# K's builds with low positions as weights, K's rows moved inside SBUF, and a new written-out order

## The chip, the cores and the metric

The kernel runs on one core of one Trainium2 chip. The metric is device time of one execution in microseconds (us), the median of three runs. A profiled execution of the kernel before gives the trace; its times are counted from the first instruction of the span.

## The reference

Two independent results stand side by side in one output of 2048 x 896 (bfloat16).

The first 448 columns are linear attention with 16 heads of 28: `qkv = x @ wqkv`; q and k go through a head's 28 x 28 matrix, then both softmaxes of it and of its negative make 56 features; the output is `phi_q (phi_k^T v) / (phi_q sum(phi_k))`, times `wo`.

The last 448 columns are a long convolution. For each of 448 channels a filter K of 2048 positions is a sum over 256 complex states, and the signal u is convolved with it:

```python
P = jnp.exp(logdA[:, :, None] * l[None, None, :])
K = jnp.einsum("dn,dnl,dn->dl", Cc, P, dB).real
...
Yf = Uf * Kf[None, :, :, :]
y = irfft2(Yf)[..., :L] + u * Dskip
```

`logdA` and `dB` come from the inputs by `dt = exp(log_dt)`. The positions `l` are rounded to bfloat16, so that large ones repeat.

## The kernel before, in words

**Stages.** The signal's spectrum is made by matmuls with tables (`signal_spectrum`, L593) and parked in DRAM. Attention runs as 16 key tiles (`key_tile`, L742), an end of the keys (`key_end`, L774), and four query stretches (`query`, L784) of 512 rows. K is made in eight blocks of 56 channels (`NCHK`), in three groups (`GROUPS`, L36: blocks 0 to 3, then 4 and 5, then 6 and 7). When a group's K is there, its spectrum follows (`kernel_spectrum`, L864), then the product with the signal's spectrum (`conv_group`, L948) and the inverse (`inverse`, L921).

**How a block of K is made.** A position is a high part (32 values, `HI`) plus a low part (49 values, `LO`), so K at (h, lo) is a sum over states of U at h times W at lo. `dampings` and `rotations` make W for the 49 low positions with ScalarE's exponentials and sines, after groups of 16 matmuls (`phases`); `damp` multiplies the two on VectorE. `hi_tables` (L698) makes U for the 32 high positions in five levels, each two products and a sum. The sum is an accumulating DMA that GpSimd issues for the (block, level) pairs in `ADD_BY_DMA` (L97: blocks 1 to 6), and otherwise an add on VectorE. `build_k` (L723) then makes one block in two builds of 112 matmuls: for each of 7 channels, four terms (two halves of the states, real and imaginary) and four groups g of channels, with U's 32 high positions as weights and W's 49 low positions streaming, each group in a tile of 32 columns of the array (`tile_position=(0, 32 * g)`). A build's 128 x 343 result is evicted into `Ts`, whose partition is 32g + h and whose free axes are lo and channel. Both operands of a build's matmul are read with a step of a whole row of 112 or 224 elements.

**How K's rows are put in place.** The spectrum wants `Kt`: 5 tiles of 128 partitions, one partition a position, in the order `K_ROWS` (L33) gives. `scatter_k` (L842) writes the group's `Ts` to a DRAM tensor `KD` by four DMAs (step `kd`), then reads `KD` back into `Kt` by eight DMAs and into `KZ` by two (step `sc`), and multiplies one row of `KZ` (step `last`). DMAs go out on SyncE's or GpSimd's queue.

**What sets the order.** Nothing is scheduled on the chip or by the compiler: each operation is a unit with a number, and `ORDER` (L100) lists all units with the engine each runs on (P, D, A, G, S for TensorE, VectorE, ScalarE, GpSimd, SyncE). `HOMES` (L158) fixes the bytes of each tile in SBUF and `BANKS` the PSUM bank of each result. A search made these lists from the costs that the helpers carry (`tt`, `act`, `copy`, `dma`: L327 to L382); the costs have no other effect. Waits follow from the data, and each engine takes its own units strictly in the listed order. All vector operations have the line of their helper: L330 products and sums, L340 activations, L350 evictions, L359 matmuls, L381 DMAs.

Of the kernel before, what the change touches and what calls it, by code (L numbers as in the profile page):

```python
# [9 lines left out]
BF16 = mybir.dt.bfloat16  # L10
# [10 lines left out]
NQ = 14  # L21
CW = 4 * NQ
# [10 lines left out]
K_ROWS = [(0, 0, 0, 8, (9, 25, 1), 1), (1, 0, 0, 8, (25, 41, 1), 1), (2, 0, 8, 16, (10, 41, 2), 1), (3, 0, 16, 24, (1, 8, 1), 0),  # L33
          (3, 56, 16, 24, (8, 41, 4), 0), (4, 0, 24, 32, (0, 8, 2), 0), (4, 32, 24, 32, (8, 41, 8), 0), (4, 72, 24, 32, (41, 48, 1), 0)]
# [9 lines left out]
def _row_positions():  # L44
    pos = {}
    for kt, r, h0, h1, run, low_first in K_ROWS:
        hl = [(h, lo) for h in range(h0, h1) for lo in range(*run)]
        if low_first:
            hl = [(h, lo) for lo in range(*run) for h in range(h0, h1)]
        for i, (h, lo) in enumerate(hl):  # L50
            pos[kt, r + i] = HI[h] + LO[lo]
    return pos
# [44 lines left out]
ADD_BY_DMA = {(k, lv) for k in range(1, 7) for lv in range(5)}  # L97
# [3 lines left out]
15G 0S 24P 8A 154G 1A 85P 2S 5S 81P 4A 25A 26D 87P 6S 88D 199G 27P 23D 86D 83P 7A 49P 84D 3A 33A 16G 82D 51P 29A 34D  # L101
155G 19G 54P 52A 56D 153S 50A 31A 57D 53P 30A 58D 156D 10S 13S 12S 60D 32A 55D 59D 157D 28P 38A 41A 37A 46A 43A 35A
44A 97P 190P 168P 40A 39D 47A 169A 18S 183P 664P 113P 36D 98A 184A 665A 45D 175P 667A 666A 200G 42D 99P 100A 115P 116D
176A 48D 669A 198S 160P 161A 119P 193P 120D 61D 101P 661P 194A 102D 668A 191A 114A 62D 662A 201D 195P 196A 131P 170P
663A 64D 171A 172S 69A 173P 158P 174A 185P 197S 132D 71A 9S 117P 240P 241A 238P 239A 135P 63D 186A 70A 73D 75A 210P
202D 72D 136D 66D 133P 118A 211A 20G 178P 89P 93P 159A 162S 94A 205P 103P 104D 179A 21S 220P 22S 65D 76A 206A 90D 230P
78D 74A 203P 77D 204A 129P 221A 130D 228P 231A 229A 232S 68D 67D 79A 180P 95P 682S 163P 673P 96D 127P 80A 181A 728S
134D 208P 209A 683D 730D 681A 212S 684D 218P 729D 242S 680A 225P 226A 698G 91P 223P 164A 678A 685D 687D 676A 128A 188P
189A 731G 686D 674A 92D 215P 192S 688D 137P 213P 224D 216A 207S 214A 732D 139P 733D 219A 233P 234A 235P 222S 677A 236A
141P 679A 138A 690D 689D 675A 165P 691D 693D 701D 123P 140A 124A 700D 166A 125P 187S 692D 126A 142A 237S 694D 143P  # L110
734G 736D 144A 670P 671A 696D 121P 716P 122A 177S 735D 717A 243P 276P 167S 718A 672A 227S 246A 265P 268A 182S 245A
695D 699D 702D 707P 709A 708A 11S 710P 697D 737G 739D 738D 740G 217S 775D 821D 254P 257A 279A 711A 256A 719P 713A 267A
705P 703P 278A 712A 765P 715A 14S 714A 726A 720A 249D 250D 744G 723A 722A 774S 721A 769A 724A 260D 105P 727A 790G 282D
742D 725A 244P 248A 770A 776D 704A 777G 283D 766A 706A 741D 266P 743G 17G 773A 261D 753P 247G 771A 762P 746D 106D 745D
779D 768A 767A 269G 772A 309P 778D 780G 270A 748D 747D 763A 271D 764A 756P 758A 749P 751P 251D 755A 782D 781D 783G
760A 750D 761A 754A 312A 972D 255P 107P 757A 791D 752A 822D 253P 108A 311A 298P 259A 820S 109P 110A 300A 301A 272D
258G 299P 792D 303A 799P 287P 793D 800A 784D 759A 785D 262D 252P 273D 823G 289A 824D 825D 304D 786G 801A 111P 826G
263P 264P 787D 802P 290A 302G 788D 321P 794D 112A 805A 291G 274P 325A 803A 320P 275P 288P 828D 277P 310P 323A 293D
804A 315D 806A 807A 281A 322A 314A 292A 827D 811P 789G 313G 305D 818A 817A 316D 829G 294D 808P 795P 815A 810A 797P
814A 809A 306D 971S 962P 295D 812A 838D 317D 796A 280G 284D 286P 297P 973D 974G 285P 813A 296P 967A 819A 326D 308P  # L120
963A 970A 830D 831D 307P 318P 964A 354P 816A 837D 975D 959P 966A 965A 358A 976D 798A 836G 832G 968A 397P 319P 324G
969A 961A 327D 343P 833D 960A 328D 950P 834D 840D 347A 951A 977G 365P 839D 952A 369A 332P 978D 331P 979D 334A 835G
333A 337D 953P 957A 956A 1018D 958A 988D 841P 400A 954A 843P 335G 842A 399A 338D 401G 955A 980G 999P 403D 1019D 844A
353P 1001A 1017S 1000A 355A 982D 981D 329P 847S 336A 342P 356A 989D 375P 991D 378A 983G 1002A 990D 398P 402A 1004A
357G 339D 985D 377A 984D 1003A 408P 1020G 411A 364P 330P 340P 341P 387P 410A 367A 344A 845G 345A 391A 386P 389A 996P
997A 376P 998A 409P 1021D 1022D 368G 414D 388A 846G 366A 359D 346G 348D 1008P 413A 360D 392D 1005P 1010A 986G 349D
1009A 380A 370D 1014A 1023G 1024D 848G 987G 1025D 1006A 1007A 381D 1026G 992P 993A 361D 994P 404D 1129D 1119P 350D
351P 352P 415D 1130D 1016A 371D 382D 995A 393D 1013A 1116P 390G 363P 1012A 1121A 405D 412G 379G 1122A 1011A 372D 362P
373P 1027D 1128S 145S 383D 374P 385P 1015A 1127A 1033G 428P 1028D 1131G 1126A 1124A 1120A 152S 1144G 394D 396P 407P
1035D 1029G 384P 425P 395P 1118A 151S 1133D 851G 849S 416D 1132D 1123A 1134G 1117A 1125A 418P 406P 1034D 417P 881S  # L130
426A 1153P 1107P 1030D 1155A 1031D 1154A 1032G 1109A 427A 1037D 1156P 1108A 1036D 858G 431P 430A 1136D 1135D 893S
1110P 429A 1038P 420D 1137G 432A 1115A 433A 1112A 1146D 1111A 1158A 422D 1114A 863S 419D 1039A 1113A 1175D 1157A 1040P
423D 852G 424D 1160A 1174S 1145D 1176D 1161A 1139D 1159A 434P 435A 489P 1041A 492P 490A 1138D 1140G 453P 486P 436A
455P 494A 547P 1147D 1043S 443P 421D 454A 493A 437P 1044S 1148D 850S 1141D 880S 1142D 465P 491A 456A 473P 856G 463P
444A 488A 855G 464D 487A 475P 859D 466A 438D 439D 440D 1177D 1179D 1178D 854G 476A 483P 899S 1143G 857S 485A 484A 905S
1162P 474A 1045G 853G 1180D 445P 446A 513P 1165P 1172A 1181D 514A 1169A 874S 1164A 495P 1163A 904S 1149P 496D 1151P
862S 1182D 497D 887S 1042S 521P 1166A 522A 1150A 882P 869S 1183D 1168A 1184D 883A 1170A 864P 1185D 441D 1186D 886S
442D 892S 1167A 898S 894P 1152A 888P 1187D 1173A 1188D 875S 1051S 477D 1171A 1055G 531P 532A 876P 889A 865A 1047S 906P
907A 868S 895A 877A 884P 503P 504A 1192D 501P 502A 885A 1050G 861S 908P 900P 870P 871A 890P 1053S 909A 1046S 523P 533P
150S 891A 1052G 146S 1054G 511P 498D 512A 1048S 1191D 872P 860G 550P 901A 1189D 896P 897A 534A 1049S 1193D 1190G 878P  # L140
879A 1194D 552A 551A 1056D 524A 478P 1195P 1196A 1197P 479A 902P 1198A 1200G 499D 1201G 500D 903A 515D 548A 447D 866P
1199S 602P 603A 910D 535D 536P 537A 149S 549A 604A 505D 867A 599P 911D 1202S 1204S 1212G 1206S 1211G 467D 147S 525D
526P 600A 148S 544P 457D 458P 873A 912D 545A 448P 449A 1207G 601A 913D 459A 516P 541P 468P 469A 929D 930D 517A 1205S
527A 1203G 608P 542A 605P 1071P 610A 1210G 543A 1072A 916D 928D 1063P 1064A 1067P 506P 1208S 914D 931D 1213D 1068A
1065P 559P 480P 1059P 915D 609A 932D 1066A 481A 546A 606A 607A 518P 507A 933D 935D 528P 450P 451A 519A 1073P 529D 553P
1074A 934D 1060A 1057S 569P 1224P 570A 936D 659S 452S 1239D 470P 1209S 1061P 1062A 937D 1069P 471A 1070A 1220P 1221A
1216P 1217A 554D 591P 592A 917D 1228P 555D 556D 1058G 538P 1222P 460P 1225A 658S 589P 1082D 561P 657S 1223A 1226P
1218P 557D 1229A 461A 462S 938D 1230P 1076D 1219A 560A 520S 558D 923P 571P 508P 509A 562D 1231A 1227D 581P 1075D 563D
660S 582A 1077D 1078D 918P 590A 919A 572A 1215G 939D 593D 925P 1091D 1214G 579P 580A 583D 564P 1089D 942P 1080D 1100D
926A 617P 618A 1092D 539A 584P 945P 924A 1232D 947P 510S 565A 573D 1093D 948A 482S 1233D 920P 1235D 639P 1081D 574P  # L150
575A 566P 567A 1086P 1079D 585A 472S 627P 1234D 1237D 628A 1238D 1087A 640A 594P 595A 576P 586P 946A 649P 927S 587A
1236D 1240P 1241A 1249D 647P 940P 921A 1090D 1243P 568S 1094D 1095D 1096D 1099D 1097D 1101P 577A 578S 1247D 1251D 922S
# [124 lines left out]
def kernel(  # L277
# [65 lines left out]
    def acopy(out_, a):  # L343
        sbuf = 0 if isinstance(a, tuple) else 0.045
        plan.add({"ACT": 0.039 + sbuf + count(out_) * 0.8333e-3}, lambda e: nc.scalar.copy(at(out_), at(a)), [whose(a)], [out_])  # L345
# [696 lines left out]
```

## Time and profile before

| what | before |
|---|---|
| median of 3 runs | 311.49 us (311.19 to 312.22) |
| the profiled execution | 313.22 us, span 311.3 us |
| TensorE busy | 251.5 us, 4152 matmuls |
| VectorE busy | 265.3 us, 334 instructions |
| ScalarE busy | 239.8 us, 417 instructions |
| GpSimd busy | 55.2 us, 93 instructions |
| mean granted TensorE clock | 0.950 |
| DMA packets | 50233, 41.11 MB; 32467 under 512 bytes |

A row of a group reads: line, engine (PE TensorE's matmuls, PEld its weight loads, DVE VectorE, ACT ScalarE, POOL GpSimd, SP SyncE), operation, what it writes and reads, shapes and count, then busy time in us and the mean of one in ns, then the idle time of the engine just before and what ended it. For a matmul, 128*32 means 128 rows and 32 columns of weights. In rows of stretches, each engine has its busy us and in brackets the number of instructions alive in the stretch; then the granted clock, the share of the DMA engines and GB/s. In the chain of waits, each row has a start, a length and what took that time. In rows of DMA issues: count, KB each, median us to landing.

### The profile page before, as it was taken

What the parts mean: (1) busy time and instruction counts of PE and PEld (TensorE: products, weight loads), DVE (VectorE), ACT (ScalarE), POOL (GpSimd) and SP (SyncE); (2) the same over time, 40 slices, a digit from 0 to 9 for tenths busy, and PEclk for the clock granted to TensorE, in tenths of its full rate; (3) what the DMA queues carried; (4) which work ended last, traced back from release to release, by engine and by line L of the source; (5) the groups of instructions that cost most, each with busy time, mean ns of one, the idle gap of its engine ahead of it and who ended that gap; (6) DMA issues with size and microseconds to landing.
All of it is one profiled execution on the core that took longest, in us unless ns stands there. A gap on an engine that the chain in (4) does not pass through costs nothing.

```text
span 311.3 us, 9636 instructions
## 1 busy us (share of the span) xinstructions
PE 251.5 (81%) x4152; PEld 202.6 (65%) x4152; DVE 265.3 (85%) x334; ACT 239.8 (77%) x417; POOL 55.2 (18%) x93
## 2 busy tenths in 40 slices
PE   4539787966968989779997793999993999699994
PEld 3524454444847667475686672989973688588982
DVE  1399999989999898999999993979985977699683
ACT  2698999999999998988999992869793475307342
POOL 3003000111231222315332240230113310000000
PEclk9987999999799999999999997799998799879999
DMA  7684432786363645457957569569092896310254
GB/s 242 175 270 155 138 117 60 193 264 150 85 115 73 114 91 113 83 107 123 142 98 148 106 111 113 120 151 286 9 50 33 187 355 184 129 29 17 76 135 133
DMA packets 50233, 41.11 MB, mean 132 GB/s; under 512 B 32467, under 2 KB 46336, under 8 KB 49808
## 3 DMA queue, kind: packets, MB, share of 16 engines
q1 hardware_dynamic: 42384, 24.50, 30.7%
q0 software_dynamic: 6128, 14.83, 25.2%
q10 hardware_dynamic: 1680, 1.18, 1.4%
q8 instruction: 32, 0.52, 0.7%
q14 instruction: 9, 0.07, 0.1%
HBM read 20.29 MB, written 8.74 MB: 93 GB/s over the span
## 4 chain that ended last, share of the span: by engine, by line
PE 26%; DVE 20%; DMA 19%; ACT 7%; issue 5%; SPq 2%; DVEq 0%; ACTq 0%
PE psum L359 26%; DVE sbuf L330 18%; DMA sbuf<-sbuf 9%; ACT sbuf L340 4%; DMA KD<-sbuf 3%; DMA sbuf<-const 3%; ACT sbuf L350 2%; DMA out_dram<-sbuf 2%; SPq L381 2%; DVE sbuf L758 1%; DMA sbuf<-in_A_wo_dram 1%; DVE sbuf L764 1%; ACT L340 0%; DVE sbuf L806 0%; DVE sbuf L809 0%
## 5 line engine op out<-in xcount | busy, mean ns | idle before, releaser
L359 PE MATMUL psum<-sbuf 128*32 128x49 bf16 (+10 forms) x4056 | 247.1, 262 | 50.0 <-ACT sbuf L350 13.4
L359 PEld LDWEIGHTS <-sbuf 128*32 128x32 bf16 (+5 forms) x4056 | 195.4, 122 | 95.8 <-issue 48.2
L330 DVE TENSOR_TENSOR sbuf<-sbuf 128x896 bf16<-128x896 bf16 (+8 forms) x241 | 218.2, 954 | 32.9 <-DMA sbuf<-sbuf 8.9
L340 ACT ACTIVATE sbuf<-psum 128x448 bf16<-128x448 f32 (+4 forms) x213 | 137.4, 773 | 2.7 <-PE psum L359 2.6
L350 ACT CAST sbuf<-psum 128x448 bf16<-128x448 f32 (+3 forms) x171 | 90.1, 600 | 56.2 <-PE psum L359 49.9
L381 POOL DMA_DIRECT2D sbuf<-sbuf x30 | 25.7, 870 | 102.1 <-DVE sbuf L330 56.3
L340 ACT ACT_TABLE_LOAD x13 | 16.7, 1283 | 2.3 <-issue 2.1
L758 DVE TENSOR_REDUCE sbuf<-sbuf 128x32 f32<-128x896 bf16 x16 | 16.7, 1065 | 0.0
L381 POOL DMA_DIRECT2D sbuf<-KD x16 | 10.6, 706 | 21.1 <-DMA KD<-sbuf 21.1
L330 DVE TENSOR_TENSOR sbuf<-psum,sbuf 128x896 f32<-128x896 f32 (+4 forms) x14 | 9.0, 660 | 4.9 <-PE psum L359 4.6
L564 PE MATMUL psum<-sbuf 128*112 128x128 bf16 x64 | 6.7, 242 | 5.9 <-DMA sbuf<-in_A_x_dram 2.8
L564 PEld LDWEIGHTS <-sbuf 128*112 128x112 bf16 x64 | 6.1, 149 | 7.6 <-DMA sbuf<-in_A_x_dram 4.6
L350 DVE CAST sbuf<-psum 128x448 bf16<-128x448 f32 (+2 forms) x13 | 8.0, 629 | 2.0 <-PE psum L359 1.2
L381 POOL DMA_DIRECT2D KD<-sbuf x6 | 7.2, 1297 | 13.9 <-ACT sbuf L350 13.8
L695 POOL MEMSET sbuf<- 128x224 bf16 x8 | 3.8, 479 | 23.1 <-DVE sbuf L330 19.1
L350 DVE COPY sbuf<-psum 112x512 bf16<-112x512 bf16 (+1 forms) x16 | 6.3, 406 | 1.7 <-PE psum L564 1.5
L603 POOL DMA_INDIRECT sbuf<-in_B_u_dram,sbuf x2 | 3.2, 1593 | 25.3 <-DVE sbuf L330 25.1
L381 POOL DMA_DIRECT2D sbuf<-SUd x4 | 4.7, 1182 | 8.8 <-PE psum L359 6.4
L753 POOL MEMSET sbuf<- 128x16 bf16 x16 | 5.8, 451 | 2.5 <-DMA sbuf<-sbuf 2.5
L345 ACT CAST sbuf<-sbuf 128x1792 bf16<-128x1792 f32 x3 | 5.7, 1899 | 0.0
L350 ACT COPY sbuf<-psum 112x512 bf16<-112x512 bf16 (+1 forms) x8 | 5.2, 648 | 0.3 <-PE psum L564 0.3
L764 DVE RECIPROCAL sbuf<-sbuf 128x32 bf16<-128x32 f32 x16 | 5.0, 334 | 0.1
(20 smaller groups left out, 30.4 us busy)
## 6 DMA issues: line engine op xcount, KB each, us to landing
sbuf<-sbuf POOLq DMA_DIRECT2D x12, 448.0 KB, 4.4
sbuf<-sbuf POOLq DMA_DIRECT2D x18, 224.0 KB, 3.8
SUd<-sbuf SPq DMA_DIRECT2D x16, 224.0 KB, 2.1
sbuf<-const SPq DMA_DIRECT2D x3, 1024.0 KB
sbuf<-const SPq DMA_DIRECT2D x17, 160.0 KB, 4.3
out_dram<-sbuf SPq DMA_DIRECT2D x24, 112.0 KB, 4.8
sbuf<-sbuf SPq DMA_DIRECT2D x8, 224.0 KB
sbuf<-in_B_u_dram SPq DMA_DIRECT2D x2, 896.0 KB
```

Source lines behind the costliest of these rows:

```text
L330: lambda e: nc.vector.tensor_tensor(out=at(out_), in0=at(a), in1=at(b), op=op), [whose(a), whose(b)], [out_])
L340: lambda e: nc.scalar.activation(at(out_), at(a), func, scale=scale, bias=bias), [whose(a)], [out_],
L345: plan.add({"ACT": 0.039 + sbuf + count(out_) * 0.8333e-3}, lambda e: nc.scalar.copy(at(out_), at(a)), [whose(a)], [out_])
L350: lambda e: (nc.scalar.copy if e == "ACT" else nc.vector.tensor_copy)(at(out_), at(a)), [whose(a)], [out_])
L359: nc.tensor.matmul(out_, lhsT=lhsT, rhs=rhs, start=start, stop=stop, **kw)
L381: plan.add({e: own[e] for e in engs}, lambda e: QUEUES[e].dma_start(out=out_, in_=in_, **kw), r, w, mode=k, load=wire, lat=(1.0 if dram el ...
L564: mms(p, [lambda t, j=j, x=x: nc.tensor.transpose(t[:, j, :], x[:, 112 * j:112 * j + 112], ident[:, :]) for j in range(4)], 0.22, [x, iden ...
L603: plan.add({"POOL": 1.2}, lambda e: nc.gpsimd.indirect_dma_start(out=ub.rearrange("p s d -> p (s d)"), out_offset=None, in_=u8, in_offset= ...
L695: pool(0.2, lambda en: nc.gpsimd.memset(w[:, :, ZERO, :], float(np.sqrt(0.5))), [], [w[:, :, ZERO, :]])
L753: pool(0.2, lambda e: nc.gpsimd.memset(V[:, D_HEAD, :], 1.0), [], [V[:, D_HEAD, :]])
L758: plan.add({"DVE": 0.996}, lambda e: nc.vector.tensor_reduce(zk[:, :, :], EK[:, :, :].rearrange("p s (h f) -> p s h f", f=D_HEAD), axis=AX ...
L764: nc.vector.reciprocal(rk[:, :, :], zk[:, :, :])
```

## The change

- **Builds.** The operands change sides: W's 49 low positions are the weights, U's 32 high positions stream. `NQ` is 28 instead of 14, so that a block has two groups g of 28 channels instead of four of 14, each in a tile of 64 columns of the array. A build takes 14 channels instead of 7, still with 112 matmuls. Its result is 113 x 448, and `Ts` has partition 64g + lo and free axes h and channel.
- **K's rows.** `KD` is gone. Each of the 8 entries of `K_ROWS` goes for each of the two g straight from `Ts` to `Kt` by a DMA inside SBUF, and five more fill `KZ`: 21 for a group, where 14 were.
- **Sums by DMA.** `ADD_BY_DMA` now holds blocks 0 and 7 too, and group 0's two sums of products in `conv_group` are accumulating DMAs.
- **Costs, order, places.** The costs in the helpers are a few ns higher (VectorE 0.061 to 0.068 and the like); small DMA pieces cost 1.3 times as much there; a build's cost is left at 2.75. `ORDER`, `HOMES` and `BANKS` are new. Units on TensorE stay 315; VectorE has 337 (334 before), ScalarE 390 (409), GpSimd 111 (89), SyncE 132 (117).

```diff
-NQ = 14
-CW = 4 * NQ
+NQ = 28
+CW = 2 * NQ
...
-ADD_BY_DMA = {(k, lv) for k in range(1, 7) for lv in range(5)}
+ADD_BY_DMA = {(k, lv) for k in range(8) for lv in range(5)}
...
     def build_k(k, Ts, x0):
+        half = NQ // 2
         for hq in range(2):
             step(f"build{k}.{hq}")
-            p = ps([128, 7, N_LO])
+            p = ps([113, half, N_HI])
             calls = []
-            for qq in range(7):
-                q = 7 * hq + qq
+            for qq in range(half):
                 for i in range(4):
                     nch, ri = i // 2, i % 2
-                    for g in range(4):
-                        xc = nch * CW + g * NQ + q
+                    for g in range(2):
+                        xc = nch * CW + g * NQ + half * hq + qq
                         calls.append(lambda t, g=g, qq=qq, i=i, ri=ri, xc=xc: mm(
-                            t[32 * g:32 * g + 32, qq, :], U[k][:, :, ri, xc], W[k][:, ri, :, xc], i == 0, i == 3,
-                            tile_position=(0, 32 * g)))
+                            t[64 * g:64 * g + N_LO, qq, :], W[k][:, ri, :, xc], U[k][:, :, ri, xc], i == 0, i == 3,
+                            tile_position=(0, 64 * g)))
             mms(p, calls, 2.75, [U[k], W[k]], mode=1)
-            copy(Ts[:, :, x0 + 7 * hq:x0 + 7 * hq + 7], (p, lambda t: t.rearrange("p c l -> p l c")))
+            x = x0 + half * hq
+            copy(Ts[:, :, x:x + half], (p, lambda t: t.rearrange("p c h -> p h c")))
...
     def scatter_k(gi, Ts):
-        step(f"kd{gi}")
+        step(f"sc{gi}")
         c0, n = GROUPS[gi]
+        x = NQ * n
+        for g in range(2):
+            cs_ = slice(c0 * CW + x * g, c0 * CW + x * g + x)
+            for kt, r, h0, h1, (l0, l1, s) in K_ROWS:
+                d = Kt[r:r + (h1 - h0) * len(range(l0, l1, s)), kt, cs_]
+                dma(["SP", "POOL"], d, Ts[64 * g + l0:64 * g + l1:s, h0:h1, :], r=[Ts], w=[d])
+        step(f"last{gi}")
         cs_ = group_cols(gi)
-        x = NQ * n
-        for g in range(4):
-            v = Ts[32 * g:32 * g + 32, :, :]
-            dma(["SP", "POOL"], KD[gi][:, :, x * g:x * g + x].rearrange("l h x -> h l x"), v, r=[v], w=[("KD", gi, g)])
-        step(f"sc{gi}")
-        kd = [("KD", gi, g) for g in range(4)]
-        for kt, r, h0, h1, (l0, l1, s), low_first in K_ROWS:
-            m = (h1 - h0) * len(range(l0, l1, s))
-            d = Kt[r:r + m, kt, cs_]
-            v = KD[gi][l0:l1:s, h0:h1, :]
-            dma(["SP", "POOL"], d, v if low_first else v.rearrange("l h x -> h l x"), r=kd, w=[d])
         d = KZ[0:1, cs_]
-        dma(["SP", "POOL"], d, KD[gi][8, 0:1, :], r=kd, w=[d])
+        dma(["SP", "POOL"], d, Ts[8:73:64, 0, :], r=[Ts], w=[d])
         d = KZ[32:36, cs_]
-        dma(["SP", "POOL"], d, KD[gi][48, 31:32, :].to_broadcast([4, CW * n]), r=kd, w=[d])
-        step(f"last{gi}")
+        for j in range(4):
+            dma(["SP", "POOL"], KZ[32 + j:33 + j, cs_], Ts[48:113:64, 31, :], r=[Ts], w=[KZ[32 + j:33 + j, cs_]])
         tt(d, d, U4[32:36, cs_], ALU.mult)
...
         for i in range(2):
-            tt(a[i][:, :, :], a[i][:, :, :], c[i][:, :, :], ALU.add)
+            if gi == 0:
+                dma(["POOL"], a[i].rearrange("p a b -> p (a b)"), c[i].rearrange("p a b -> p (a b)"), r=[c[i]], w=[a[i]],
+                    max_dma_last_dim=3584, accum_op=ALU.add)
+            else:
+                tt(a[i][:, :, :], a[i][:, :, :], c[i][:, :, :], ALU.add)
         finish(1, *a)
```

More of the change, by code (lines that the diff above doesn't have):

```diff
@@ L45, in _row_positions @@
     pos = {}
[L46 to L50, printed above, removed]
+    for kt, r, h0, h1, run in K_ROWS:
+        for i, (lo, h) in enumerate((lo, h) for lo in range(*run) for h in range(h0, h1)):
             pos[kt, r + i] = HI[h] + LO[lo]
@@ L104 @@
[L104 to L113, printed above, removed]
@@ L199 @@
+6060207202036541254226737433735221545606020022672731367210251622004004206043441662322"
 class Plan:
@@ L338, in act @@
         sbuf = 0 if isinstance(a, tuple) else 0.045
-        plan.add({"ACT": 0.05 + sbuf + count(out_) * 0.8333e-3},
+        plan.add({"ACT": 0.056 + sbuf + count(out_) * 0.8333e-3},
                  lambda e: nc.scalar.activation(at(out_), at(a), func, scale=scale, bias=bias), [whose(a)], [out_],
@@ L344, in acopy @@
         sbuf = 0 if isinstance(a, tuple) else 0.045
-        plan.add({"ACT": 0.039 + sbuf + count(out_) * 0.8333e-3}, lambda e: nc.scalar.copy(at(out_), at(a)), [whose(a)], [out_])
+        plan.add({"ACT": 0.045 + sbuf + count(out_) * 0.8333e-3}, lambda e: nc.scalar.copy(at(out_), at(a)), [whose(a)], [out_])
     def copy(out_, a, rate=1.0417e-3):
         n = count(out_)
-        plan.add({"ACT": 0.039 + n * 0.8333e-3, "DVE": 0.065 + n * rate},
+        plan.add({"ACT": 0.052 + n * 0.8333e-3, "DVE": 0.07 + n * rate},
                  lambda e: (nc.scalar.copy if e == "ACT" else nc.vector.tensor_copy)(at(out_), at(a)), [whose(a)], [out_])
```

136 lines of the change are left out of this document (72 added, 64 removed), and 63 rows, old and new, of the table HOMES.

## The prediction

> **What bounds the kernel now.** I read the page's head first, then the busy time of the engines in stretches cut at the kernel's own marks: the first build of K (77.77 us), the first build of the last block (218.09), the last build's end (223.87), the end.
>
> ```profile
> PE 251.5 (81%) x4152; PEld 202.6 (65%) x4152; DVE 265.3 (85%) x334; ACT 239.8 (77%) x417; POOL 55.2 (18%) x93
> ```
>
> ```profile
> core 0: us, PE busy (x) PEld busy (x) DVE busy (x) ACT busy (x) POOL busy (x), PEclk, DMA share, GB/s
> 0.00:77.77 77.77, 53.20 (x452) 35.18 (x452) 64.64 (x72) 67.43 (x103) 8.44 (x16) 0.96 0.59 177
> 77.77:218.09 140.32, 117.71 (x2480) 98.24 (x2480) 128.38 (x168) 125.92 (x221) 38.48 (x67) 0.96 0.64 121
> 218.09:223.87 5.78, 5.78 (x227) 5.62 (x226) 5.78 (x6) 4.37 (x8) 0.00 (x0) 1.00 0.01 3
> 223.87:311.32 87.45, 74.77 (x996) 63.56 (x996) 66.50 (x91) 42.06 (x87) 8.23 (x10) 0.92 0.51 119
> sum 311.32, PE 251.46 PEld 202.59 DVE 265.30 ACT 239.78 POOL 55.15; mean PE 62.86 PEld 50.65 DVE 66.33 ACT 59.94 POOL 13.79
> ```
>
> No engine bounds all of it. In the middle stretch VectorE (128.4 of 140.3 us) and ScalarE (125.9) set the pace and TensorE has 22.6 us to spare; in the tail TensorE is the busiest with 74.8 of 87.5. So work added to TensorE is free in the middle until it has used those 22 us, and is paid in full afterwards. How close TensorE can come to fully busy, a denser stretch shows:
>
> ```profile
> 200.00:224.00 24.00, 23.44 (x578) 22.33 (x568) 21.91 (x30) 18.94 (x38) 3.77 (x6) 1.00 0.63 166
> ```
>
> That is 0.977, which I take as its ceiling. Last, the chain of waits (start, length, what) and the list of waits (total, times, longest), for what the trip of K through DRAM costs:
>
> ```profile
> 226.79 10.33 DMA KD<-sbuf
> ```
>
> ```profile
> PE psum L359 <- DMA sbuf<-in_A_wo_dram: 5.4, 2, 5.0
> ```
>
> The last group's write to DRAM stands in the chain with 10.3 us, but TensorE has other work then and stops for only 5.4 us (the wo load it names was issued on SyncE between K's transfers and landed behind them).
>
> **The builds, step by step.** Every block of K is two builds of 112 small matmuls: 16 x 112 = 1792. Before, four 32-column tiles of the array each hold 32 high positions as weights, and 49 low positions stream past. After, the sides are swapped: 49 columns of weights need a 64-column tile, so only two tiles fit, and 32 columns stream. The count stays 1792. What one costs depends on what bounds it now.
>
> ```profile
> L359 PE MATMUL psum<-sbuf 128*32 128x49 bf16 x1792 | 46.2, 279 | 7.0 <-DVE sbuf L330 2.5 <-DMA sbuf<-sbuf 1.7 <-issue 1.6
> L359 PEld LDWEIGHTS <-sbuf 128*32 128x32 bf16 x1792 | 43.8, 141 | 8.8 <-DVE sbuf L330 4.5 <-issue 4.0
> L359 PE MATMUL psum<-sbuf 128*128 128x112 bf16 x1016 | 59.2, 216 | 7.5 <-ACT sbuf L340 6.3 <-ACT sbuf L350 0.5 <-DMA sbuf<-const 0.3
> L359 PEld LDWEIGHTS <-sbuf 128*112 128x112 bf16 x256 | 17.6, 132 | 6.2 <-issue 2.9 <-DVE sbuf L330 1.2
> L359 PE MATMUL psum<-sbuf 112*128 112x8 bf16 x128 | 3.8, 166 | 0.0
> ```
>
> A 49-column matmul lasts 279 ns, a 112-column one 216, an 8-column one 166: by the last two a column costs 0.48 ns and 49 should last 186. The 93 ns more are the build's own, as are a load of 32 columns at 141 ns against 112 columns at 132. Both operands of a build are read one element at a time, 224 or 448 bytes apart. Next, the beginning of one build in slices of some 10 ns (x counts the matmuls alive), and whole builds at two granted clocks:
>
> ```profile
> 94.52:94.53 0.01, 0.00 (x1) 1.00 0.00 0
> 94.53:94.54 0.01, 0.01 (x4) 1.00 1.83 358
> 94.54:94.59 0.05, 0.05 (x4) 1.00 1.82 358
> 94.59:94.60 0.01, 0.01 (x4) 1.00 0.00 0
> 94.60:94.61 0.01, 0.01 (x5) 1.00 3.66 717
> ...
> 94.63:94.65 0.02, 0.02 (x8) 1.00 0.91 179
> ...
> 77.77:80.50 2.73, 2.73 (x113) 2.73 (x116) 2.73 (x5) 2.73 (x6) 1.14 (x2) 0.65 0.53 149
> ...
> 94.50:97.20 2.70, 2.67 (x113) 2.70 (x116) 2.70 (x4) 2.69 (x4) 0.00 (x0) 1.00 0.11 20
> ```
>
> Four matmuls, one for each tile, start within 20 ns; then nothing starts for 60 ns, until the first tile takes its next. So the queue can hand out matmuls much faster than they run, and a tile's own chain (load, stream, next) is the limit. A build takes 2.7 us, 24.1 ns a matmul, 96.4 ns for one round of four tiles. It takes 2.73 us at a granted clock of 0.65 too, so the round isn't array cycles; it looks like reading.
>
> The swap leaves a round's reading as it was: 49 columns on one side, 32 on the other. With two tiles a round yields two matmuls: 96.4 / 2 = **48.2 ns**. The bounds: 24.1 if the tiles share something that serves one matmul after another whatever the tiles (or 15.7, 24.1 x 32/49, if that is the stream alone); 64 if the load's 17 further columns lengthen the round by 93/49 = 1.9 ns each (32 ns, so 128.7 / 2). I take 48.2, nearest to the slices, which show a chain for each tile. That is +24.1 ns for each of 1792: 43.2 us more of TensorE.
>
> The Trainium skill speaks on both sides. TensorEngine Tiling (Array Packing), Theoretical Speedup, gives up to 4x for a small dimension of at most 32 and up to 2x for at most 64; with half the tiles that is 48 ns as well, and no run here shows a 64-column tile yet. Its opposite is a rival below.
>
> **The other edits.** Durations from the forms of VectorE and the issues:
>
> ```profile
> L330 DVE TENSOR_TENSOR sbuf<-sbuf 128x1792 bf16<-128x1792 bf16 x68 | 72.2, 1085 | 10.1 <-issue 4.7 <-DMA out_dram<-sbuf 2.4 <-DMA sbuf<-sbuf 2.3
> L330 DVE TENSOR_TENSOR sbuf<-sbuf 128x896 bf16<-128x896 bf16 x106 | 61.8, 615 | 12.0 <-DMA sbuf<-sbuf 6.6 <-PE psum L359 2.7 <-DMA sbuf<-KD 1.9
> L330 DVE TENSOR_TENSOR sbuf<-sbuf 128x3584 bf16<-128x3584 bf16 x20 | 40.2, 2018 | 5.2 <-DMA KD<-sbuf 5.2
> sbuf<-sbuf POOLq DMA_DIRECT2D x12, 448.0 KB, 4.4
> L350 ACT CAST sbuf<-psum 128x343 bf16<-128x343 f32 x15 | 8.9, 592 | 2.7 <-PE psum L359 2.7
> L350 ACT CAST sbuf<-psum 128x448 bf16<-128x448 f32 x134 | 70.3, 594 | 48.6 <-PE psum L359 42.4 <-DMA sbuf<-sbuf 6.2
> ```
>
> Sums by accumulating DMA in blocks 0 and 7 take 6 x 0.615 + 4 x 1.085, those of group 0's product 2 x 2.018: 12.1 us off VectorE. Its instructions rise from 334 to 337 all the same, since 15 evictions come over from ScalarE; I cost the pair at nothing beyond the counts below. An accumulate lands after 4.4 us (448 KB) where an add took about 1; blocks 0 and 7 have other blocks' work beside them, and if that cover is gone it is five levels x 3 us, 15 us once in the middle. Group 0's two sums are of 896 KB, 4.4 to 8.8 us each. Behind the first of them on GpSimd's queue stand six moves of the last group's K, which wait for VectorE's product with it, and behind both on VectorE stands that half's finish; the group's other half and the query pieces keep TensorE busy meanwhile (cover gone: 9 us). An eviction of 448 instead of 343 columns costs the same (594 against 592).
>
> K's rows: 12 writes and 30 reads of DRAM become 63 moves inside SBUF. The writes' landing goes, and with it, I take it, the 5.4 us. From below: nothing comes back, if the 21 issues of the last group on two queues take as long; from above 10.3, the whole write. Other work is ordered there, so TensorE's own 5.4 is the nearest.
>
> **The new order**, counted by position. Before the first build VectorE now has 95 instructions instead of 75 (11 of key tiles, 4 of damping, others): 20 x 0.79 (265.3 / 334) = 15.9 us, so that build starts at 94. TensorE has moved along what it could do there: 3 phase groups of 16 matmuls at 0.058, 28 and 24 key matmuls at 0.22 and 0.074, 16 transposes at 0.105:
>
> ```profile
> L359 PE MATMUL psum<-sbuf 112*128 112x448 bf16 x192 | 42.8, 358 | 10.1 <-DMA sbuf<-in_A_wo_dram 5.4 <-ACT sbuf L350 3.2 <-ACT sbuf L340 1.4
> L359 PE MATMUL psum<-sbuf 128*112 128x116 bf16 x128 | 9.5, 214 | 2.5 <-DVE sbuf L330 2.5
> L564 PE MATMUL psum<-sbuf 128*112 128x128 bf16 x64 | 6.7, 242 | 5.9 <-DMA sbuf<-in_A_x_dram 2.8 <-DMA sbuf<-const 2.4 <-DVE sbuf L350 0.4
> L359 PE MATMUL psum<-sbuf 112*112 112x512 bf16 x64 | 16.9, 395 | 0.3 <-ACT sbuf L340 0.3
> ```
>
> together 12.5 us out of the middle. Six query groups of 4 at 0.264 and one of 8 transposes come into it from the tail, 6.9 us. VectorE's middle has 151 instructions for 161: -7.9 us.
>
> **The sum**, on the profiled execution. First build at 94. Between them: VectorE would need 140.3 - 7.9 = 132.4; TensorE needs 117.7 - 12.5 + 6.9 = 112.1, plus 14 builds x 112 x 24.1 = 37.8, 149.9 busy, 153.4 at 0.977. TensorE is the bound: the last block begins at 247.4. Its two builds: 5.8 + 5.4 = 11.2, to 258.6. Tail: 87.45 - 6.9 - 5.4 = 75.1, to 333.7. The profiled execution was 313.22 for a span of 311.32, the median of the runs is 311.49, 0.2 over that span: **334 us**, 7% slower.
>
> **The rivals.**
> 1. *A matmul stays at 24 ns* (faster). The same sum with VectorE's 132.4: 94 + 132.4 + 5.8 + 75.1 + 0.2 = 307.5. For it: 24.1 ns at both clocks, as a serving of one by one would give. Against: four starts in 20 ns. It decides up to (0.977 x 132.4 - 112.1) / 1568 = 11 ns more for each, 35 ns; above that each ns costs 1.8 us, and from 36 the kernel is slower than before. The Trainium skill has this as a rule (TensorE: Matmul & The Clock Gate, Wait — 56ns, not 53.3ns?): starts never come closer than about 25 ns however few the columns. On average this trace agrees (24.1), in the slices it doesn't.
> 2. *The round shrinks with two tiles instead of four contending for reads*, to 75 ns or so: 37 to 40 ns a matmul, 312 to 319.
> 3. *The load's further columns lengthen the round* to 64 ns: 15.8 x 1.792 / 0.977 = 29 us more, 363.
> 4. *K's moves take as long as the trip did*: TensorE stops again, +5.4 on whichever case holds.
>
> **How the numbers follow.** 48 ns, 322 to 348: 0.58. Rival 2, with 311 to 322: 0.14. Rival 1, 304 to 311: 0.22. Rival 3: 0.06. Range 305 to 346, which leaves out most of rival 3 and the edges. A measurement of this kernel tells 0.3% from no change: faster 0.22, within it 0.05 (rival 2's lower end), slower 0.73.
>
> **What would show it.** The group of build matmuls at some 85 us instead of 46.2, and 5 to 6 us a build; TensorE near 295 us and over 0.95 busy from the first build on, VectorE waiting for it; the first build at about 94; no TensorE stop on K's transfers. I am wrong if builds still take 2.7 us, or if the middle stays VectorE's.

## The result, and the profile after

The change takes 370.66 us (median of 4 runs, 369.45 to 372.49) where the kernel before took 311.37: a ratio of 1.190, 95% interval [1.184, 1.197]. That is slower, as forecast, but 25 us beyond the upper end of the range. The profiled execution was 371.62 us for a span of 369.5 us.

The head of the profile after, and its busy time in stretches cut at the same marks as before: the first build, the first build of the last block, the last build's end.

```profile
PE 306.1 (83%) x4152; PEld 255.8 (69%) x4152; DVE 262.0 (71%) x337; ACT 236.7 (64%) x402; POOL 69.1 (19%) x115
```

```profile
core 0: us, PE busy (x) PEld busy (x) DVE busy (x) ACT busy (x) POOL busy (x), PEclk, DMA share, GB/s
0.00:100.49 100.49, 67.03 (x569) 45.70 (x569) 77.72 (x89) 81.87 (x128) 17.75 (x33) 0.92 0.66 173
100.49:272.99 172.50, 160.02 (x2398) 139.63 (x2396) 117.94 (x158) 118.00 (x199) 41.81 (x69) 0.76 0.43 90
272.99:283.48 10.49, 10.49 (x225) 10.49 (x224) 6.82 (x8) 1.30 (x3) 1.21 (x1) 0.69 0.64 161
283.48:369.50 86.02, 68.54 (x970) 60.02 (x968) 59.53 (x84) 35.58 (x74) 8.34 (x12) 0.92 0.47 118
```

The middle has grown from 140.3 to 172.5 us, TensorE is now its busiest engine (160.0), and its granted clock there fell from 0.96 to 0.76. The tail is 86.0 us long although TensorE has only 68.5 us of work in it. The groups of the builds:

```profile
L356 PE MATMUL psum<-sbuf 128*49 128x32 bf16 x1792 | 86.1, 265 | 0.7 <-DVE sbuf L327 0.4 <-ACT sbuf L337 0.3
L356 PEld LDWEIGHTS <-sbuf 128*49 128x49 bf16 x1792 | 85.2, 192 | 2.6 <-issue 2.3
```

86.1 us are 48.0 ns each, the 48.2 of the forecast. VectorE's list of waits, and one of these waits in its timeline, show what the forecast lacked:

```profile
DVE sbuf L327 <- PE psum L356: 24.1, 6, 5.5
DVE sbuf L327 <- ACT sbuf L337: 15.9, 9, 3.6
DVE sbuf L802 <- DMA sbuf<-sbuf: 12.8, 2, 9.2
```

```profile
300.14 0.96 DVE L802 RECIPROCAL sbuf<-psum 128x128 f32<-128x128 f32 x1 [9.23 <-DMA sbuf<-sbuf]
```

L802 is the reciprocal of a query stretch's denominators. It reads PSUM and writes a small tile of its own. Nothing that a DMA brings is in it, and yet it stands 9.23 us for DMAs inside SBUF. TensorE in the same window (288 to 302 us) has one stretch of matmuls that ends at 295.8 and then nothing. In its own list of waits VectorE has come to the top; the longest wait for a transfer is now one for a load of inputs near the start, and of transfers inside SBUF 0.9 us are left:

```profile
287.82 7.94 PE L356 MATMUL psum<-sbuf 128*128 128x112 bf16 x156
```

```profile
PE psum L356 <- DVE sbuf L327: 24.5, 12, 7.5
PE psum L568 <- DMA sbuf<-in_A_wqkv_dram: 9.7, 1, 9.7
...
PE psum L356 <- DMA sbuf<-sbuf: 0.9, 1, 0.9
```

### The profile page after: what moved, and what is told of

Its sections match the earlier page's. It is cut to its first block, busy times and chain, and to the rows that moved or that the text cites. A ratio compares the mean times of both kernels' runs of the same rounds, so it can differ in the third digit from the quotient of the medians.

```text
span 369.5 us, 9732 instructions
## 1 busy us (share of the span) xinstructions
PE 306.1 (83%) x4152; PEld 255.8 (69%) x4152; DVE 262.0 (71%) x337; ACT 236.7 (64%) x402; POOL 69.1 (19%) x115
## 3 DMA queue, kind: packets, MB, share of 16 engines
q0 software_dynamic: 8608, 21.33, 28.5%
## 5 line engine op out<-in xcount | busy, mean ns | idle before, releaser
L356 PE MATMUL psum<-sbuf 128*49 128x32 bf16 (+8 forms) x4056 | 300.2, 263 | 46.6 <-DVE sbuf L327 24.5
L356 PEld LDWEIGHTS <-sbuf 128*49 128x49 bf16 (+4 forms) x4056 | 248.3, 148 | 94.8 <-issue 54.9
L327 DVE TENSOR_TENSOR sbuf<-sbuf 128x896 bf16<-128x896 bf16 (+7 forms) x229 | 205.7, 951 | 50.0 <-PE psum L356 24.1
L347 ACT CAST sbuf<-psum 128x448 bf16<-128x448 f32 (+3 forms) x159 | 80.2, 571 | 80.3 <-PE psum L356 75.0
L378 POOL DMA_DIRECT2D sbuf<-sbuf x76 | 59.5, 858 | 236.0 <-DVE sbuf L327 106.0
L347 DVE CAST sbuf<-psum 128x448 bf16<-128x448 f32 (+2 forms) x25 | 15.4, 629 | 7.7 <-PE psum L356 7.6
L802 DVE RECIPROCAL sbuf<-psum 128x128 f32<-128x128 f32 x4 | 3.8, 954 | 13.8 <-DMA sbuf<-sbuf 12.8
L568 PE MATMUL psum<-sbuf 112*112 112x112 bf16 x32 | 3.4, 280 | 10.6 <-DMA sbuf<-in_A_wqkv_dram 9.7
L568 PEld LDWEIGHTS <-sbuf 112*112 112x112 bf16 x32 | 3.1, 192 | 10.9 <-DMA sbuf<-in_A_wqkv_dram 9.9
L331 DVE SCALAR_TENSOR_TENSOR sbuf<-sbuf 128x64 f32<-128x64 f32 (+2 forms) x7 | 4.1, 591 | 7.1 <-DMA sbuf<-sbuf 7.1
```

The costliest lines, as they stand in the source:

```text
L327: lambda e: nc.vector.tensor_tensor(out=at(out_), in0=at(a), in1=at(b), op=op), [whose(a), whose(b)], [out_])
L347: lambda e: (nc.scalar.copy if e == "ACT" else nc.vector.tensor_copy)(at(out_), at(a)), [whose(a)], [out_])
L356: nc.tensor.matmul(out_, lhsT=lhsT, rhs=rhs, start=start, stop=stop, **kw)
L378: plan.add({e: own[e] for e in engs}, lambda e: QUEUES[e].dma_start(out=out_, in_=in_, **kw), r, w, mode=k, load=wire, lat=(1.0 if dram el ...
L568: mms(p, [lambda t, j=j: nc.tensor.transpose(t[:, 112 * j:112 * j + 112], Wqk[:, j, c0:c0 + 112], id112) for j in range(4)], 0.35, [Wqk[:, ...
```

## The experiments

On the chips of these runs the kernel before takes 314 to 315 us; the change takes 370.4 there (e13). So times are compared with other runs of this section, and ratios are to the kernel before beside them. The edits are shown shortened; what of the reference a run leaves out is said with it.

**e1: the kernel before, its builds on two tiles.** The old sides stay; half of K is overwritten by the other half.

```diff
-for i in range(4): for g in range(4): tile 32 * g
+for gh, i in ...: for gt in range(2): tile 64 * gt, channel group 2 * gt + gh
```

> The kernel before, its order and its 1792 build matmuls of 32 columns of weights and 49 streaming, but on two tiles of the array instead of four: the second pair of groups of each channel is written over the first, so half of K is lost. Theory (a tile works through load and stream one after the other, some 94 ns, and only the number of tiles sets the rate): 47 to 48 ns a matmul, build group 84 to 88 us, granted clock falling to 0.5 within each pair of builds, other matmul groups some 10 us dearer, 345 to 360 us. Rival (the 49 columns as weights are what is slow): builds stay at 24 ns, 311 us. Rival (four tiles contend, two run shorter rounds): 37 to 40 ns, 320 to 330 us.

Measured: 349.56 us, ratio 1.113 [1.104, 1.122].

```profile
L359 PE MATMUL psum<-sbuf 128*32 128x49 bf16 x1792 | 86.3, 276 | 4.4 <-DVE sbuf L330 3.4 <-issue 1.0
```

```profile
78.14:248.86 170.72, 151.85 (x2481) 133.19 (x2482) 128.88 (x168) 126.36 (x221) 38.47 (x67) 0.96 0.53 99
```

Two tiles alone nearly double the builds (46.2 to 86.3 us), as a chain for each tile would have it. The granted clock, which was expected to fall within the builds, stayed at 0.96. The middle grew by 30.4 us (140.3 to 170.7), though TensorE seemed to have 22.6 to spare for its 34 more: by the forecast's rule, 117.7 + 34.1 at 0.977, it should have grown by 15. I take it that in an order made for short builds the slack, spread over many places, isn't there where a long build needs it; no run tried that by itself.

**e2: the change, its builds back on four tiles.** As before, 32 columns of weights and 49 streaming (K's values are not in their places); order, moves and sums are the change's.

```diff
-t[64 * g:64 * g + N_LO, qq, :], W[k][:, ri, :, xc], U[k][:, :, ri, xc], ... tile_position=(0, 64 * g)
+t[32 * g:32 * g + 32, qq, :], U[k][:, :, ri, xc], W[k][:, ri, :, xc], ... tile_position=(0, 32 * g)
```

> The changed kernel with the builds' matmuls alone put back: 32 high positions as weights on four tiles, 49 streaming, evicted from a part of the result in the changed kernel's shape, so K's rows are wrong. Theory (the builds and the low clock that follows them make the loss): 24 ns a matmul, granted clock at 0.93 or more, other matmul groups back at some 205 us, 303 to 312 us. Rival (the new order, the moves inside SBUF or the accumulating DMAs are slow by themselves): first build still at about 100 us, tail of 80 us or more with TensorE idle for over 15 us, 318 to 330 us.

Measured: 337.16 us, ratio 1.076 [1.066, 1.086], beyond the theory and the rival. With builds at their old price the rest of the change is 23 us slower than before, where the forecast had 4 us faster. So the builds aren't the whole story. Its VectorE waits:

```profile
DVE sbuf L803 <- DMA sbuf<-sbuf: 16.3, 3, 7.1
DVE sbuf L327 <- DMA sbuf<-sbuf: 12.3, 9, 5.4
...
DVE sbuf L331 <- DMA sbuf<-sbuf: 7.2, 3, 4.2
```

**e3: the change, each build matmul split in 32 and 17 columns**, so that four tiles are used: 3584 matmuls. It computes all of the reference.

```diff
+for l0, l1 in ((0, 32), (32, N_LO)):
-    t[64 * g:64 * g + N_LO, qq, :], W[k][:, ri, :, xc], ...
+    t[64 * g + l0:64 * g + l1, qq, :], W[k][:, ri, l0:l1, xc], ... tile_position=(0, 64 * g + l0)
```

> The changed kernel with each build matmul split in two: the low positions' 49 columns of weights as 32 and 17, on tiles 0 to 3 in turn, the same 32 columns streaming, the same result; 3584 matmuls. Theory in its first form (a tile's load and stream cost by their columns, some 1.16 ns each): rounds of 57 to 74 ns, four matmuls in one, 16 to 18 ns a matmul, 2 x 112 in 3.6 to 4 us a build, 335 to 345 us. In its second form (a load and a stream cost some 47 ns each whatever their columns): 94 ns a round, 23.5 ns, 5.2 us a build, 370 us as the changed kernel. Rival (starts never closer than some 25 ns on average): 5.6 us a build, 375 us or more.

Measured: 386.38 us, ratio 1.225 [1.214, 1.237]. It is no cure. The first build of it, in one stretch, and what its matmuls waited for in the whole run:

```profile
98.27:102.70 4.43, 3.86 (x226) 3.74 (x228) 4.43 (x9) 4.43 (x8) 0.85 (x1) 1.00 0.26 48
```

```profile
PE psum L356 <- issue: 34.6, 24, 4.2
```

In its busy time a build costs what the theory's first form gave: 3.86 us for 224 matmuls, 17.2 ns each. But the time is 41 us beyond that form's range: twice the instructions bring stops in which TensorE waits for nothing but its own issue, 34.6 us in all, where the change's list of TensorE's waits, down to 0.4 us, has no such row. The last section looks at these stops.

**e4: the kernel before, builds reading neighbouring elements** instead of one every 224 or 448 bytes (K is then made of other elements; the matmuls have the same sizes).

```diff
-U[k][:, :, ri, xc], W[k][:, ri, :, xc]
+U[k][:, 4 * qq + g, ri, 0:N_HI], W[k][:, ri, 4 * qq + g, 0:N_LO]
```

> The kernel before with its builds' operands read as 32 and 49 neighbouring elements instead of one in 112 or 224, so K is wrong. If reading single elements far apart sets the round: loads and streams get shorter, 12 ns a matmul or less, builds of 1.4 us, 300 to 308 us since VectorE and ScalarE bound the middle. If a tile's load and stream have a fixed length, or starts keep 24 ns apart: 24 ns a matmul as before, 311 us.

Measured: 314.13 us, ratio 0.997 [0.992, 1.002]. The head, and one build:

```profile
PE 230.1 (74%) x4152; PEld 180.4 (58%) x4152; DVE 264.7 (85%) x334; ACT 240.3 (77%) x417; POOL 55.1 (18%) x93
```

```profile
114.68:115.56 0.88, 0.88 (x113) 0.88 (x112) 0.88 (x2) 0.88 (x1) 0.00 (x0) 1.00 0.40 74
```

112 matmuls in 0.88 us are 7.9 ns each instead of 24.1. So the round of 96 ns was mostly reading, and no least distance of 24 ns holds. The time stayed above the 300 to 308 that were expected: 21 us less TensorE time (230.1 against 251.5) brought nothing. About 10 of them came back as stops in which TensorE waits for its own issue (11.5 us against 1.6 before); that the rest brought nothing either agrees with VectorE and ScalarE as the bound before, but this run doesn't show it by itself.

**e5: e2 without stepped sources.** Half of the entries of `K_ROWS` are moved from every second, fourth or eighth partition of `Ts`, and `KZ`'s rows from partitions 64 apart. Here they read as many neighbouring partitions; count, bytes and queues stay (so K's rows hold other positions).

```diff
+l1, s = l0 + len(range(l0, l1, s)), 1
-Ts[8:73:64, 0, :]      Ts[48:113:64, 31, :]
+Ts[8:10, 0, :]         Ts[48:50, 31, :]
```

> The kernel is e2_after_four_tiles (the change with its builds on four tiles, 337.2 us) with one more edit: the moves of K that take every second, fourth, eighth or 64th partition of Ts take as many neighbouring partitions instead (K's rows are then wrong ones; count, bytes and queues of the moves are as before). Theory (unneeded waits): in the trace of e2 VectorE stands 28 us in all before query units that write neither Ts nor Kt, and what they wait for is each time a move with a stepped source. With the steps gone these waits go, and the time falls by 15 to 25 us, to 312 to 322. Rival (the order itself is the cost): the same units wait as long for TensorE's sums or for K, and the time stays at 333 to 338.

Measured: 305.52 us, ratio 0.967 [0.958, 0.976]: 31.6 us off e2, more than the theory's 15 to 25, and now faster than the kernel before. In VectorE's list no reciprocal waits for a DMA any more, and the other lines have shrunk:

```profile
DVE sbuf L331 <- DMA sbuf<-sbuf: 1.1, 1, 1.1
DVE sbuf L327 <- DMA sbuf<-sbuf: 1.0, 2, 0.7
```

The waits are written in the program, not made by the chip. The first such reciprocal in the change, and in the change without stepped sources:

```
L802 Reciprocal [waits DMAHW2, DMAHW3, DMAHW1, DMAHW4, DMAHW0, DMAHW5, DMASW6, DMAHW6, DMASW1, Activation]
L802 Reciprocal [waits Activation]
```

I read this so: where a DMA's source has a step between partitions, the program builder takes it to touch bytes that it doesn't touch, and makes later writers of those bytes wait until the move has landed. That inner reason was not tried by itself; that the waits come and go with the steps is shown: in the built programs 84 of VectorE's instructions wait for a DMA in the change, and 73 without the steps, as in the kernel before. So "waits follow from the data", as it stands ahead of the prediction, isn't the whole of it. Nor are moves with a step slower themselves: those of 7.9 KB on GpSimd's queue land after 2.7 us in the change and after 4.5 without steps (e9).

**e6: e5, with the weight fold reading the identity**, so that it waits for no load.

```diff
-Wqk[:, j, c0:c0 + 112], id112)
+ident[0:112, 0:112], id112)
```

> e5_rest_unit_steps with one more edit: the 32 transposes that fold the query and key weights read the identity instead of the loaded weights, so that they don't wait for that load (all products with the folded weights are wrong; the instructions are the same). Theory (front): the 9 us in which TensorE, VectorE and ScalarE all stand at the beginning of e2 go, the first build starts some 9 us earlier (89 instead of 98) and the time falls by 7 to 10 us below e5. Rival (covered): what VectorE and ScalarE have to do before the first build sets its start, and the time is within 3 us of e5.

Measured: 305.57 us, no change from e5. TensorE's longest wait of the front in e5, and in e6:

```profile
PE psum L568 <- DMA sbuf<-in_A_wqkv_dram: 8.7, 1, 8.7
```

```profile
PE psum L356 <- DMA sbuf<-in_B_C_re_dram: 8.6, 1, 8.6
```

The load issued next, that of `C_re`, takes the place of the one removed, to 0.1 us. By these two rows the front waits for the inputs as a whole.

**e7: e2 with K's trip through DRAM put back**, two writes and ten reads a group in the places of the moves.

```diff
-Kt[...] <- Ts[64 * g + l0:64 * g + l1:s, h0:h1, :]   (16 and 5 a group)
+KD[gi] <- Ts (2 a group), Kt[...] and KZ[...] <- KD[gi] (10 a group)
```

> e2_after_four_tiles with K's trip through DRAM put back: each group's 21 moves inside SBUF become 2 writes to DRAM and 10 reads, in the same places of the order. By the theory of unneeded waits, a source in DRAM has no stepped partitions in SBUF, VectorE's waits go, and the time is that of e5 plus about the 5 us that TensorE stood for the trip in the kernel before: 315 to 327. By the rival (the order itself is the cost) it stays at 337 or rises by those 5 us to 342. If the moves inside SBUF were worth what the prediction gave them, this run would be some 5 us slower than e2.

Measured: 327.08 us, ratio 1.039 [1.030, 1.048], at the upper end of what the theory gave. So in this order the moves inside SBUF are 10 us worse than the trip with their unneeded waits (e2), and 21.6 us better without them (e5).

**e8 and e14: two tiles, but 49 columns streaming**, in the change (e8) and in e9 (e14); half of K is left out. They are told together, behind e9.

**e9: the change itself without stepped sources** (e5's edit).

> The change itself with only the stepped sources of K's moves taken away (as many neighbouring partitions instead, so K's rows are wrong ones); its builds stay on two tiles with 32 columns streaming. Theory (two separate causes that add up): the unneeded waits cost what they cost between e2 and e5, 31.6 us, and the builds what they cost between e2 and the change, 33.5 us; then this run is 370.7 - 31.6 = 339.1, say 335 to 343. Second theory (the builds' 43 us of TensorE time are paid in full once nothing else waits): 305.5 + 43 = 348.5, 345 to 352. Rival (the waits were only visible because nothing else was late, and with two tiles the builds cover them): 355 or more.

Measured: 347.22 us, ratio 1.107 [1.097, 1.117]; the second theory. It is 23.2 us less than the change (e13), and 41.7 more than e5, which differs from it by the builds alone.

> The change (370.7 us) with its builds still on two tiles, but with the old sides: 32 columns of weights, 49 streaming, half of K left out; the count of 1792 stays. Both take about 47 ns a matmul (46.9 and 47.2 were measured), but with 32 streaming the granted clock fell to 0.5 in each pair of builds, with 49 it did not. Theory (the low clock is a cost of its own, since the matmuls behind a pair run at half clock): the clock returns to about 0.95, the other matmuls lose some 12 us of busy time, and the time falls to 356 to 364. Rival (the engines wait for the builds and not for the matmuls behind them): the clock returns, and the time stays at 367 to 373.

> e9_after_unit_steps (347.2 us, granted clock 0.854) with the old sides on its two tiles: 32 columns of weights, 49 streaming, 47 ns a matmul as before, half of K left out. With the unneeded waits gone TensorE is the bound, so what the low clock costs must show now. Theory (the matmuls behind a pair of builds run at half clock, and that is paid): the clock returns to 0.93 or more and the time falls by 6 to 12 us, to 335 to 341. Rival (the low clock falls into waits): 344 to 349.

Measured: e8 367.11 us, ratio 1.165 [1.158, 1.172], as the rival had it; e14 339.16 us, ratio 1.077 [1.069, 1.085], as the theory had it. The middle of e9, then of e14, then of e5, which differs from e14 by the number of tiles:

```profile
98.98:264.15 165.17, 157.70 (x2399) 137.56 (x2397) 118.59 (x158) 118.60 (x200) 42.73 (x70) 0.77 0.46 94
```

```profile
97.37:253.39 156.02, 146.79 (x2396) 128.37 (x2396) 118.38 (x158) 117.77 (x200) 42.67 (x70) 0.98 0.48 100
```

```profile
98.34:225.89 127.55, 114.21 (x2396) 94.67 (x2397) 117.53 (x158) 117.15 (x200) 42.73 (x70) 0.96 0.59 122
```

In e9 and e14, the 1792 build matmuls are busy for 86 to 87 us, and VectorE and ScalarE have the same work to within 1 us. What differs is the clock, 0.77 against 0.98, and with it TensorE's other matmuls: 10.9 us of busy time and 9.2 us of the stretch. In the times it is 8.1 us (347.2 to 339.2). In the change itself, where VectorE's waits cover part of it, it is 3.3 (370.4 to 367.1).

**e10: the change's order, sums and moves, with the old sides in the builds.** With 32 high positions as weights a partition of `Ts` is a high position, and no move needs a step between partitions; they are half-sized and twice as many. It computes all of the reference.

```diff
-Kt[...] <- Ts[64 * g + l0:64 * g + l1:s, h0:h1, :]     for g in range(2)
+Kt[...] <- Ts[32 * g + h0:32 * g + h1, l0:l1:s, :]     for g in range(4)
```

> The change's order, accumulating DMAs and moves inside SBUF, but with the old sides in the builds (32 high positions as weights, 49 low ones streaming, four tiles), so that a partition of Ts is a high position and no move has a stepped source: 16 pairs of half-sized moves for each group and 8 for the rows of KZ. It computes all of the reference. Theory (order, accumulates and moves are worth about 9 us together, and only builds and stepped sources spoilt them): 300 to 309, faster than before, some us beside e5's 305.5. Rival (the moves' issues, twice as many, on SyncE's and GpSimd's queues are late for the last group): 310 to 318, no gain over before.

Measured: 309.39 us, ratio 0.984 [0.977, 0.992]. It beats the change by 61 us and the kernel before by 1.6%, an interval that stays below 1 though a gain of 2% isn't shown. It is 3.9 us above e5. In its built program no reciprocal of a query stretch waits for a DMA.

**e11: e5 with the twelve sums back on VectorE. e12: the kernel before with only those sums given to DMAs.**

```diff
-ADD_BY_DMA: blocks 0 to 7, and group 0's two sums
+ADD_BY_DMA: blocks 1 to 6            (e11; e12 is the reverse in the kernel before)
```

> e5_rest_unit_steps with the sums that the change gave to accumulating DMAs (blocks 0 and 7, and the two of group 0's product) back as VectorE's adds in the same places of the order. Theory (VectorE's 12.1 us are worth most of themselves): 305.5 + 6 to 12, 311 to 318. Rival (the adds' places are covered, or the accumulates' landing costs as much): within 3 us of e5, 302 to 308.

> The kernel before (314 us on this chip) with one part of the change alone: the same twelve sums by accumulating DMA in the places where VectorE added. It computes all of the reference. Theory: VectorE's middle falls by some 5.8 us and its tail by 6; in an order that was made for adds most of it is given back, since what follows waits for a landing of 4.4 us instead of an add of 1: 308 to 314. Rival (paid in full as time): 300 to 306. Third (landing dearer than the adds): above 316.

Measured: e11 306.68 us, ratio 0.975 [0.968, 0.982], 1.2 more than e5 and little more than the noise, as its rival had it; e12 344.83 us, ratio 1.092 [1.082, 1.103], as the third case had it. VectorE's waits for DMAs inside SBUF, in the kernel before and in e12:

```profile
DVE sbuf L330 <- DMA sbuf<-sbuf: 8.9, 6, 5.1
```

```profile
DVE sbuf L330 <- DMA sbuf<-sbuf: 51.8, 15, 11.3
```

An accumulate in the place of an add is no free add: in an order made for adds the twelve cost 30 us, in the change's order nothing. I take it that this one puts other work behind them. The first build, at 77.8 us before, comes at 89.7 in e12.

**e13: the change once more**, beside the kernel before on the chip of e14.

> The change itself once more, beside the kernel before on the same chip as the next run, because the kernel before takes 1% longer on the chips of the experiments (314 to 315 us) than on that of the first comparison (311.4). If the change scales with it, it takes 373 to 376 us here, and the unneeded waits are worth 26 to 29 us in the two-tile kernel (against 347.2 in e9); if it doesn't, 369 to 372, and they are worth 22 to 25.

Measured: 370.39 us, ratio 1.174 [1.166, 1.183]. It doesn't scale with the kernel before.

## Why the prediction was wrong

From the medians of these runs the time can be stepped through, one difference at a time: kernel before 314.2; order, sums and moves, -8.7 (e5, 305.5); builds on two tiles at full clock, +33.6 (e14, 339.2); the low clock, +8.1 (e9, 347.2); the unneeded waits, +23.2 (e13, 370.4). The forecast's own sum against the profiled stretches, in us:

| stretch | forecast | e14 | e9 | the change |
|---|---|---|---|---|
| to the first build | 94 | 97.4 | 99.0 | 100.5 |
| middle | 153.4 | 156.0 | 165.2 | 172.5 |
| last block's builds | 11.2 | 10.5 | 10.5 | 10.5 |
| tail | 75.1 | 70.1 | 69.5 | 86.0 |
| span | 333.7 | 334.0 | 344.1 | 369.5 |

So the sum was that of a kernel without two things that this one has. That it meets e14's span to 0.3 us is partly luck: its parts miss by 3.4, 2.6, -0.7 and -5.0 us, and the profiled execution of e14 is its fastest (336.0; the median is 339.2, 5 us above the forecast).

- **The price of a build was right**: 48.0 ns for 48.2 (46.1 by the length of a build, 5.16 us), by a tile's own chain. Rivals 1 to 3 (24, 37 to 40 and 64 ns) fell. The forecast had the chain from slices alone: e4 makes the reading its main cause, and e1 shows that halving the tiles by itself nearly doubles the builds.
- **The step that failed first is the one on K's rows**: "The writes' landing goes, and with it, I take it, the 5.4 us", and behind it "no TensorE stop on K's transfers". Its bounds, 0 and 10.3 us back, and rival 4, took for granted that only readers of K wait for the moves. To the letter TensorE's own stop on K's transfers did go (0.9 us left). In its place stand waits of VectorE's instructions that neither read nor write K, and TensorE behind them: 23.2 us in the change, 31.6 with short builds. Between e9 and the change they lengthen the tail by 16.5 us and the middle by 7.3; one row has 9.23 us of the tail, in which TensorE, too, runs out of work. In the new order the moves themselves, without such waits, are worth 21.6 us against the trip through DRAM (e5 against e7); that order was made for moves, so this is no measure of the 5.4.
- **The second is a step that was not there**: the sum took every other matmul at the durations of before, and 0.977 from a stretch at clock 1.00. That the builds would change the clock wasn't asked. It costs 8.1 us in e9 and 3.3 in the change, and TensorE's total came to 306.1 us for "near 295" (284.8 in e14).
- **"Work added to TensorE is free in the middle until it has used those 22 us"** fails in the order of before (e1: 30 us paid of 34). In the new one the sum's 153.4 us came close to e14's 156.0, but by two misses that offset each other: TensorE was busy for 146.8 us instead of 149.9, and for 0.94 of the stretch instead of 0.977. Against e5, whose TensorE has 13.3 us to spare in the middle, 28.5 us were paid of 32.6. So in neither order did the builds get the slack that a stretch's busy time shows; it is a bound from below.
- **The other edits** came to -8.7 us instead of -4.0, the smallest miss. The reasons were partly others: the sums gave 1.2 (e11), and the tail was 5 us shorter than forecast (70.1 for 75.1), while the first build came 3 to 7 us later than the 94 forecast. VectorE's work before it rose by 13.1 us, less than the 15.9 counted; its waiting, which the count left out, rose by 9.6, and one wait of 9.7 us in it is for matmuls that wait for the load of wqkv.
- The causes don't simply add. The builds cost 33.2 us with the waits there (e2 to e13) and 41.7 without (e5 to e9); the clock 3.3 and 8.1. A run that takes one cause away from the full change undersizes it by what the other covers.

## What to carry to other kernels

A transfer's price is also who waits for it: read in the built program what each instruction waits for, and doubt any wait on a DMA whose data the instruction doesn't touch; a step between a source's partitions was enough for 23 to 32 us here, and a layout in which the moved rows are neighbours (e10) removed it. Where each tile works through a chain of its own, half the tiles cost nearly twice the time (46.2 to 86.3 us here), and the slack that an engine shows over a stretch is no credit for longer pieces: 30 of 34 us were paid in an order made for short builds, and 28.5 of 32.6 in the new one. A sum moved to an accumulating DMA needs an order that has other work behind it: the same edit was worth 1 us in one order and cost 30 in another.

## What the runs showed of the hardware

**Single elements, far apart, set a small matmul's pace.** A build went from 24.1 to 7.9 ns a matmul by reading neighbours instead of elements 224 and 448 bytes apart (e4). The Trainium skill (Advanced Engine Details and Errata, SBUF Cachelines) says that a different line of 16 bytes for each access costs; this case agrees, with a factor of three. The Trainium skill's least distance of about 25 ns between starts (TensorE: Matmul & The Clock Gate, Wait — 56ns, not 53.3ns?), which the prediction weighed, doesn't hold for four tiles: 7.9 ns in e4.

**A queue full of matmuls doesn't keep the clock up.** The two builds of the first pair in the change, and the other matmuls that follow them:

```profile
100.49:105.66 5.17, 5.17 (x112) 5.17 (x112) 5.17 (x9) 5.17 (x9) 0.85 (x1) 1.00 0.25 45
105.76:110.92 5.16, 5.16 (x115) 5.16 (x114) 0.00 (x0) 2.07 (x4) 0.00 (x0) 0.56 0.02 4
110.93:114.66 3.73, 3.73 (x42) 3.52 (x40) 3.43 (x6) 1.38 (x2) 1.58 (x3) 0.50 0.56 107
```

TensorE is busy throughout, and the granted clock falls to 0.5 within these 10 us of two tiles with 32 columns streaming. With 49 streaming at the same pace the middle's mean is 0.98 (e14). The build itself doesn't feel the low clock (5.17 and 5.16 us at 1.00 and 0.56); what comes behind it does. The Trainium skill (TensorE: Matmul & The Clock Gate, What's actually happening) ties the clock to how busy the array has been. These runs would agree if busy means columns streamed and not matmuls queued. That isn't shown: e9 and e14 also differ in their columns of weights, 49 and 32.

**Dense short matmuls stop at steps of 256 instructions.** In e4 and e3 TensorE stops for 1 to 4 us with nothing to wait for. In e4 the build behind the one above:

```profile
115.57:118.37 2.80, 1.13 (x134) 1.02 (x122) 2.80 (x4) 2.79 (x6) 0.00 (x0) 1.00 0.34 76
```

1.13 us of work take 2.80. The queue that brings instructions (packets, MB, share), in e4 and in e3:

```profile
q8 instruction: 32, 0.52, 0.7%
```

```profile
q8 instruction: 46, 0.75, 0.8%
```

It brings 16 KB a packet, and e3's 3584 further instructions take 14 packets more, 256 for each. The stops lie on the same grid: counted in matmuls and loads, all 20 stops over 0.7 us of e3 that end with nothing but issue lie whole multiples of 256 instructions apart, and so do all six of e4. That each is the fetch of the next 16 KB is my reading; no run tried it alone.
